# Loading the first channel chunk in DRAM's order and turning it with TensorE, in a mixer kernel on one core

## The chip, the cores and the metric

The kernel runs on one core of one Trainium2 chip. The metric is the device time of one execution in microseconds (us). The kernel before takes 663.87 us, the median of three runs (662.96 to 666.24). About 0.5%, 3.3 us, is what a measurement of this kernel can tell from no change.

The core has a matrix engine (TensorE, PE in the profile, with its weight loads shown apart as PEld), three elementwise engines (VectorE or DVE, ScalarE or ACT, GpSimd or POOL) and SyncE (SP), which here only issues DMAs. ACT and POOL can issue DMAs too. Each engine runs its own instructions in order; they wait for each other through semaphores.

## What is computed

The reference is one block with S = 2048 tokens and D = 640 channels, in float32. Only the first half of it is touched by the change:

```python
mod = (silu(c) @ w_mod).reshape(1, 6, 1, -1)          # sa, ca, ga, sb, cb, gb
h = layernorm(x) * (1 + ca) + sa                      # x = A_q
k_shift = sum over t of k_pad[:, t:t+S, :] * shift_k[:, 3 - t]   # 4 taps, causal, per channel
kv = k_shift * v
y = causal convolution over all 2048 tokens of kv with ssm_k (by FFT), + kv * ssm_D
x = x + ga * (h * y)
x = x + gb * token_mlp(layernorm(x) * (1 + cb) + sb)  # two matrix products over the tokens, gelu between
```

## The kernel before

The 640 channels are worked in five chunks of DC = 128. The long convolution of a chunk is a Fourier transform in two steps, written as matrix products. A token number is 32 * n1 + n2, with n1 below 64 and n2 below 32. Step one sums over n1, so it wants n1 on the partitions, and two halves h of 64 channels fill the 128 partitions: partition 64 * h + n1. The free dimension then holds the 32 values n2 and the 64 channels of that half. `step1` (L211) does that for both sides: side 1 is the filter `ssm_k` (in P, called KSP), side 0 is kv (in X, for the first chunk in X0, which lies in T_y). Each call of step1 handles 8 of 32 channel pairs, 16 matrix instructions of 128 columns, and ScalarE brings the result into T_z (L229). Step two is `f2` (L233): eight groups g, each 32 matrix instructions of 64 columns against W2 (the profile shows each such float32 instruction as two), then ScalarE copies one half out of PSUM (L246) and VectorE multiplies the two spectra in two instructions (`mul`, p<-pst,kt), GpSimd adds (`add`, y<-p). The way back is `i2` (L262) and `i1` (L284), then `gate` (L310).

kv is made from k and v by `kv_ops` (L179): per group of 8 of the n2 values, eight elementwise instructions of 128 x 512, on VectorE or on GpSimd. Groups 0, 2 and 3 of the first chunk are VectorE's and group 1 is GpSimd's.

In the first chunk, k, v and ssm_k are read so that they stand in step one's order at once (`load_k` L130, `load_v` L136, `load_halo` L142, `load_ks` L155). For k and v this makes runs of 64 numbers, 256 bytes, in DRAM; for ssm_k runs of 32 numbers, 128 bytes. `perm_add` (L161) adds ssm_D to the filter's first element on GpSimd, and `perm` (L167) reorders the filter in SBUF on ScalarE, in two instructions (L168).

The order is written out by hand; no scheduler moves anything. The part that matters is L450 to L700. On PE it is: ten warming products without a use (L497), four step1 of the filter, four step1 of kv, eight groups of f2, then, for the first chunk alone and partly for the second one's filter and kv: step1(0, 0), a small transpose, step1(0, 1), i2(0), step1(0, 2), i2(1), step1(0, 3), five `mod_part` (L351, the product with w_mod) and `mod_row` (L362). On VectorE it is: kv groups 0, 2 and 3 of the first chunk, kv groups 0 and 2 of the second chunk, and only then the multiplications of f2, with one instruction of the second chunk's kv group 3 between two of them; behind f2 stand 16 pieces of row statistics (L590, L591) of q. On ScalarE, `w2_part` (L485) spreads the constant W2 from its loaded form, and stands between the step1 and f2 copies.

The second chunk's k goes into KX1, which lies in T_aux; its v goes into VX, where the first chunk's v stood. The second chunk's filter (`load_ks(1)`) goes into KSR, also in T_aux, and because one of the five pieces of w_mod is loaded to the same place (`homes`), load_ks(1) stands behind the third mod_part. SyncE issues nearly all DMAs, in order: the first chunk, the second chunk's k and v between them with two halves of W2, q (into T_x[1], then into T_x[0], where W2's loaded form was), the constant V1, w_mod, then load_ks(1) and the third chunk. A DMA takes one of eight completion semaphores in turn, so an issue also waits for the DMA eight before it.

PSUM is a ring of three slots of 1024 numbers per partition for PE's results, and one more (`tap`).

Of the kernel before, what the change touches and what calls it, by code (L numbers as in the profile page):

```python
# [11 lines left out]
AF = mybir.ActivationFunctionType  # L12
# [8 lines left out]
def _constants():  # L21
# [21 lines left out]
    return {"small": small.astype(np.float32), "w2": w2.reshape(128, 4096).astype(np.float32),  # L43
# [4 lines left out]
def mixer_kernel(ctx: ExitStack, tc: tile.TileContext, q, k, v, shift_k, ssm_k, ssm_D, w1, b1, w2, b2, c,  # L48
                 w_mod, c_small, c_w2, c_v1, out):
# [39 lines left out]
    KX1 = T_aux[:, 0:2240].rearrange("p (n i) -> p n i", i=64)  # L89
# [29 lines left out]
    epsc = small(1)  # L119
# [4 lines left out]
    TAP = tap[:, 512:768].rearrange("p (s i) -> p s i", s=4)  # L124


    kx_of = lambda c: KX1 if c == 1 else KX
    ksr_of = lambda c: T_y[:, 2048:4096] if c == 0 else KSR

    def load_k(c, g, engs=(sync, sync), n=1):  # L130
        for h in range(2):
            r = slice(64 * h, 64 * h + 64)
            engs[h].dma_start(kx_of(c)[r, 3 + 8 * g:3 + 8 * (g + n)],
                           dram(k, 8 * g * D + DC * c + 64 * h, [[32 * D, 64], [D, 8 * n], [1, 64]]))
# [7 lines left out]
    def load_halo(c):  # L142
        for h in range(2):
            sync.dma_start(kx_of(c)[64 * h + 1:64 * h + 64, 0:3],
# [10 lines left out]
    def load_ks(c, upper=sync):  # L155
        for h in range(2):
            (sync, upper)[h].dma_start(ksr_of(c)[64 * h:64 * h + 64].rearrange("p (i n) -> p i n", i=64),
# [3 lines left out]
    def perm_add(c, eng=pool):  # L161
        for h in range(2):
            r = ksr_of(c)[64 * h:64 * h + 1].rearrange("p (i n) -> p i n", i=64)[:, :, 0]
            TT(eng, r, r, DR[64 * h:64 * h + 1], ALU.add)

    def perm(c):
        for i in (slice(0, 16), slice(16, 32)):  # L167
            act.activation(KSP.rearrange("p i (n e) -> p i e n", e=2)[:, i],  # L168
                           ksr_of(c).rearrange("p (i e n) -> p i e n", e=2, i=32)[:, i], AF.Copy)
# [6 lines left out]
    def kv_ops(g, eng=dve, x=X, kx_=KX):  # L176
# [6 lines left out]
        for s in (2, 1, 0):  # L183
# [3 lines left out]
                              pairs(S_), pairs(VX[:, 8 * g:8 * g + 8]), ALU.mult))  # L187
        return ops
# [264 lines left out]
    dve.memset(epsc, EPS)  # L453
    for h in range(2):
        dve.memset(KX[64 * h:64 * h + 1, 0:3, :], 0.0)
        dve.memset(KX1[64 * h:64 * h + 1, 0:3, :], 0.0)
    both = (sync, act)
    load_taps(0, act)
    load_halo(0)
    load_k(0, 0, both)  # L460
    load_k(0, 1, both)
# [3 lines left out]
    load_v(0, 0, both)  # L465
    load_k(0, 2, both)
    load_ks(0, act)
    load_v(0, 2, both)
    load_k(0, 3)
    load_v(0, 1)  # L470
    load_v(0, 3)

    def all_taps():
        for eng, t in ((pool, PW), (dve, TAP)):
            eng.tensor_scalar(t, TR.rearrange("p (i s) -> p s i", s=4), 1.0, None, op0=ALU.mult)
# [17 lines left out]
    all_taps()  # L493
    load_taps(1, pool)
    ps = psum()
    for _ in range(10):
        pe.matmul(ps[:, 0:512], T_in[:, 192:320], T_in[:, 192:704], start=True, stop=True)  # L497
# [898 lines left out]
```

## Time and profile before

| what | before |
| --- | --- |
| median of three runs | 663.87 us (662.96 to 666.24) |
| the profiled execution | 661.6 us, of which 659.8 us from its first to its last instruction |
| PE busy | 614.0 us, 93% |
| VectorE busy | 536.3 us, 81% |
| ScalarE busy | 327.8 us, 50% |
| GpSimd busy | 127.4 us, 19% |
| first f2 matmul begins, last one ends | 34.25 us, 54.5 us |
| first multiplication of f2 on VectorE begins | 40.47 us |
| w_mod's products on PE | 76.05 to 81.6 us |

A row of the timeline says when a stretch of like instructions begins, how long it lasts, its engine and source line, what it writes and reads (out<-in), the shapes, the number of instructions (x), and in brackets how long the engine was idle before it and what ended that. "issue" there means that the engine waited for nothing that the profile shows. Most elementwise instructions have line L57, that of a helper, so their tiles tell them apart.

### The profile page before, as it was taken

To read this page: it belongs to the slowest core of one execution; us is meant where nothing else is said; L and a number is where in the kernel's file an instruction comes from. 1 tells how busy PE (TensorE), PEld (TensorE's weight loads), DVE (VectorE), ACT (ScalarE), POOL (GpSimd) and SP (SyncE) were. 2 spreads that over 40 slices of the span, in tenths; PEclk is the share of its full clock that TensorE was granted. 3 is DMA by queue.
4 is the path that set the end of the run, shared out by engine and by line. 5 is a ranking of instruction groups with operands and counts; after the bars stand their busy time and mean duration, and the time that the engine had idled before them with its cause. 6 is when DMAs were issued, how large, how long until landed. Compare 5 with 4: busy or idle time off the path is not lost.

```text
span 659.8 us, 20943 instructions
## 1 busy us (share of the span) xinstructions
PE 614.0 (93%) x9061; PEld 582.2 (88%) x9061; DVE 536.3 (81%) x930; ACT 327.8 (50%) x534; POOL 127.4 (19%) x143
## 2 busy tenths in 40 slices
PE   6978878999999899878999999999999999999997
PEld 2867567899999897778897999999999999999997
DVE  7798689979899269889979866575899689888895
ACT  0664475746747456477885553345443143333331
POOL 5772048325035044000000000000000520000000
PEclk9999899999999899989999999999999999999999
DMA  9999898465525234160318352245932636346601
GB/s 189 213 252 252 295 185 170 112 111 134 90 68 183 67 99 155 43 142 12 65 33 225 114 147 71 64 123 164 274 92 65 195 105 183 115 120 181 183 30 40
DMA packets 173356, 88.46 MB, mean 134 GB/s; under 512 B 92270, under 2 KB 163472, under 8 KB 173264
## 3 DMA queue, kind: packets, MB, share of 16 engines
q1 hardware_dynamic: 166092, 85.53, 50.6%
q10 hardware_dynamic: 6916, 1.31, 1.1%
q8 instruction: 71, 1.16, 0.7%
q0 software_dynamic: 256, 0.28, 0.2%
q14 instruction: 21, 0.17, 0.1%
HBM read 73.01 MB, written 14.09 MB: 132 GB/s over the span
## 4 chain that ended last, share of the span: by engine, by line
PE 66%; DVE 17%; DMA 5%; ACT 5%; issue 4%; POOL 1%; SPq 1%; ACTq 0%; DVEq 0%; POOLq 0%
PE pst L1250 16%; PE pst L937 12%; PE pst L445 7%; PE pst L1327 7%; PE pst L223 7%; PE pst L271 6%; PE pst L242 6%; DVE p L57 3%; PE pst L291 2%; DVE aux L57 2%; ACT z L280 1%; PE pst L993 1%; DMA y<-in_A_ssm_k_dram 1%; PE tap L351 1%; DVE sm L548 1%
## 5 line engine op out<-in xcount | busy, mean ns | idle before, releaser
L242 PE MATMUL pst<-z,w 128*64 128x64 f32 x2560 | 78.8, 223 | 12.6 <-DVE p L57 6.9
L242 PEld LDWEIGHTS pst<-z,w 128*64 128x64 f32 x2560 | 76.7, 138 | 15.2 <-issue 10.9
L229 ACT ACTIVATE z<-pst 128x1024 f32<-128x1024 f32 (+2 forms) x45 | 43.1, 976 | 38.4 <-PE pst L223 38.3
L57 POOL TENSOR_TENSOR y<-p 128x256 f32<-128x256 f32 x72 | 51.3, 741 | 39.3 <-DVE p L57 39.1
L57 DVE TENSOR_TENSOR p<-pst,kt 128x512 f32<-128x512 f32 x80 | 50.7, 682 | 6.3 <-ACT kt L246 6.3
L271 PEld LDWEIGHTS pst<-v,y 32*128 32x128 f32 x1280 | 38.1, 187 | 5.4 <-issue 4.8
L271 PE MATMUL pst<-v,y 32*128 32x64 f32 x1280 | 40.0, 272 | 2.5 <-issue 2.3
L1250 PE MATMUL pst<-r_z,m_w 128*128 128x320 f32 x222 | 41.6, 309 | 0.1
L246 ACT ACTIVATE kt<-pst 128x512 f32<-128x512 f32 x40 | 23.9, 599 | 34.6 <-PE pst L242 18.3
L57 DVE TENSOR_TENSOR s_w<-s_w,s_w 128x768 fp32r<-128x768 f32 (+1 forms) x26 | 24.6, 947 | 19.1 <-ACT s_w L921 14.3
L223 PE MATMUL pst<-v,p 128*64 128x128 f32 x640 | 36.9, 274 | 3.2 <-ACT p L168 1.8
L921 ACT ACTIVATE s_w<-s_w 128x768 fp32r<-128x768 f32 (+1 forms) x26 | 21.8, 837 | 35.8 <-PE pst L937 12.2
L223 PEld LDWEIGHTS pst<-v,p 128*64 128x64 f32 x640 | 34.8, 137 | 4.8 <-ACT p L168 2.8
L1238 ACT ACTIVATE m_w<-m_v 128x896 fp32r<-128x896 f32 x24 | 22.7, 951 | 32.3 <-PE pst L1250 16.8
L223 PE MATMUL pst<-v,x 128*64 128x128 f32 x512 | 34.5, 291 | 4.1 <-issue 3.3
L57 DVE TENSOR_TENSOR tap<-tap,kt 128x512 f32<-128x512 f32 x51 | 35.5, 697 | 1.3
L223 PEld LDWEIGHTS pst<-v,x 128*64 128x64 f32 x512 | 31.0, 147 | 5.3 <-issue 4.7
L1250 PEld LDWEIGHTS pst<-r_z,m_w 128*128 128x128 f32 x222 | 34.8, 188 | 0.4 <-DVE m_w L57 0.4
L445 PE MATMUL pst<-r_z,wb 128*128 128x320 f32 x180 | 29.7, 323 | 4.2 <-ACT r_z L778 3.1
L445 PEld LDWEIGHTS pst<-r_z,wb 128*128 128x128 f32 x180 | 28.2, 198 | 5.5 <-ACT r_z L778 3.6
L280 ACT ACTIVATE z<-pst 128x512 f32<-128x512 f32 x38 | 20.8, 645 | 23.4 <-PE pst L271 23.4
L57 DVE TENSOR_TENSOR m_w<-m_v,m_w 128x896 fp32r<-128x896 f32 x24 | 27.9, 1167 | 3.3 <-ACT m_w L1238 2.9
(362 smaller groups left out, 1534.1 us busy)
## 6 DMA issues: line engine op xcount, KB each, us to landing
m_x<-xs SPq DMA_DIRECT2D x28, 160.0 KB
out_dram<-m_x SPq DMA_DIRECT2D x28, 160.0 KB
aux<-in_A_ssm_k_dram SPq DMA_DIRECT2D x8, 512.0 KB
m_v<-in_B_w_dram SPq DMA_DIRECT2D x9, 448.0 KB
in<-in_w_mod_dram SPq DMA_DIRECT2D x4, 960.0 KB
x<-in_B_w_dram SPq DMA_DIRECT2D x7, 448.0 KB
s_w<-in_B_w_dram SPq DMA_DIRECT2D x16, 192.0 KB
in<-in_A_v_dram SPq DMA_DIRECT2D x22, 128.0 KB
```

Of the source, the lines that this page charges most:

```text
L57: TT = lambda eng, o, a, b, op: eng.tensor_tensor(o, a, b, op=op)
L223: pe.matmul(ps[64 * ri:64 * ri + 64, o:o + 255:2], lhs, F1[:, 128 * ri:128 * ri + 128], start=True, stop=True)
L229: act.activation(Z[:, side, t, :, k0:k1], ps.rearrange("p (a k e) -> p a k e", a=4, e=2)[:, :, k0:k1], AF.Copy)
L242: pe.matmul(ps[64 * h:64 * h + 64, o:o + 64], W2[k1 // 32][:, 2 * (k1 % 32) + ri], rhs, start=True, stop=True)
L246: act.activation(kt.rearrange("p (m i) -> p m i", i=32), pv[:, :, 1], AF.Copy)
L271: pe.matmul(pp[qd // 2][:, o:o + 64], Y[p, ri, i:i + 2].rearrange("p i k -> p (i k)"), V2[p, 64 * ri:64 * ri + 64], start=ri == 0, stop=ri ...
L280: act.activation(o, i, AF.Copy)
L445: pe.matmul(ps[0:m, h, 0:320], w_.bitcast(F32R), r_[:, 320 * h:320 * h + 320].bitcast(F32R), start=first and i == 0, stop=last and i == 2)
L937: pe.matmul(o, w_.bitcast(F32R), r_.bitcast(F32R), start=first and k == 0, stop=last and k == 2)
L1238: act.activation(W[n][0].bitcast(F32R), A[p, w_], AF.Copy)
L1250: pe.matmul(bank[n], w[:, i].bitcast(F32R), r.bitcast(F32R), start=i == 0 and k == 0, stop=i == 6 and k == 2)
L1327: pe.matmul(acc[s][:, h, 0:320], w[:, f_].bitcast(F32R), u[r + h].bitcast(F32R), start=f_ == 0 and k == 0, stop=f_ == NF - 1 and k == 2)
```

## The change

The first chunk's k, v and ssm_k are loaded in DRAM's order: partition p takes the 16 tokens from 16 * p on, with 128 channels in a run of 512 bytes (`natural`, tiles KN and VN), and the filter's partition is the channel, with its 2048 numbers in a row (tile KSN). They lie in T_x[1] and T_y, not in T_in, so the second chunk's k has its usual tile KX, and the third chunk's filter buffer is no longer shared with k. The taps are loaded as 128 x 512 in place of two times 64 x 256. `kv_natural` is kv_ops in the new layout: the same eight instructions of 128 x 512 for each of the four groups, the last of which now writes over v.

The order that step one wants is then made by TensorE, with a constant TURN (an identity matrix, its even columns and its odd columns, 128 x 256): 64 matrix instructions for the filter, which replace `perm`, and 8 of 512 columns for kv. ScalarE copies both out of PSUM. The warming products are 8 in place of 10. The places of w_mod's pieces are changed, and load_ks(1) is issued behind the first two of them.

```diff
+    def natural(t, src, r, n, row, eng, p0=0, p1=128):
+        eng.dma_start(t[p0:p1, r:r + n], dram(src, (16 * p0 + row) * D, [[16 * D, p1 - p0], [D, n], [1, DC]]))
...
+    act.dma_start(T_rows[:, 0:512], dram(shift_k, 0, [[0, 128], [1, 512]]))
+    natural(KN, k, 3, 4, 0, sync)
+    natural(KN, k, 0, 3, -3, act, 1, 127)
+    natural(KN, k, 0, 3, -3, act, 127, 128)
+    natural(KN, k, 7, 4, 4, sync)
     act.activation(tm[:, 0:1], epsc, AF.Copy)
-    load_D(0, act)
+    sync.dma_start(TURN, c_turn)
+    natural(VN, v, 0, 4, 0, act)
+    sync.dma_start(KSN, dram(ssm_k, 0, [[S, 128], [1, S]]), max_dma_last_dim=2048)
+    act.dma_start(dcol, dram(ssm_D, 0, [[1, 128], [1, 1]]))
+    natural(KN, k, 11, 8, 8, sync)
     sync.dma_start(SM, dram(c_small, 0, [[422, 128], [1, 422]]))
+    natural(VN, v, 8, 4, 8, sync)
+    natural(VN, v, 4, 4, 4, sync)
+    natural(VN, v, 12, 4, 12, sync)
...
-    for _ in range(10):
-        pe.matmul(ps[:, 0:512], T_in[:, 192:320], T_in[:, 192:704], start=True, stop=True)
+    for _ in range(8):
+        pe.matmul(ps[:, 0:512], KN.rearrange("p n i -> p (n i)")[:, 384:512],
+                  KN.rearrange("p n i -> p (n i)")[:, 384:896], start=True, stop=True)
+    ops = kv_natural(1, pool)
+    run(ops[:2])
+    TT(pool, KSN[:, 0:1], KSN[:, 0:1], dcol, ALU.add)
+    run(ops[2:])
+    run(kv_natural(0))
+    run(kv_natural(2))
...
-    perm(0)
+    for b in range(2):
+        ps = psum()
+        for n in range(16):
+            for h in range(2):
+                pe.matmul(ps[64 * h:64 * h + 64, 64 * n:64 * n + 64],
+                          KSN.rearrange("p (n1 n) -> p n n1", n=32)[:, 16 * b + n], TURN[:, 64 * h:64 * h + 64],
+                          start=True, stop=True)
+        act.activation(P.rearrange("p (i n e) -> p n i e", i=32, e=2)[:, 16 * b:16 * b + 16],
+                       ps.rearrange("p (n i e) -> p n i e", n=16, e=2), AF.Copy)
...
     for t in range(4):
         step1(1, t)
     w2_part(0, 0, 0, 32)
+    for b in range(2):
+        ps = psum()
+        for n2 in range(2):
+            for h in range(2):
+                pe.matmul(ps[64 * h:64 * h + 64, 512 * n2:512 * n2 + 512], TURN[:, 128 + 64 * n2:192 + 64 * n2],
+                          VN[:, 8 * b:8 * b + 8, 64 * h:64 * h + 64], start=True, stop=True)
+        for n2 in range(2):
+            n = 16 * n2 + 8 * b
+            act.activation(X0.rearrange("p (i n e) -> p n i e", i=32, e=2)[:, n:n + 8],
+                           ps[:, 512 * n2:512 * n2 + 512].rearrange("p (n i e) -> p n i e", n=8, e=2), AF.Copy)
     for t in range(4):
         step1(0, t, x=X0, last=True)
...
-    homes = [T_v1[:, 2048:3968], T_in[:, 192:2112], T_aux[:, 0:1920], T_in[:, 2240:4160], P[:, 0:1920]]
+    homes = [T_v1[:, 2048:3968], T_aux[:, 2048:3968], T_in[:, 192:2112], T_in[:, 2240:4160], P[:, 0:1920]]
...
                     for kk in range(2):
                         mod_load(0, kk, homes[kk])
+                    load_D(1)
+                    load_ks(1)
...
-                if kk == 2:
-                    load_D(1)
-                    load_ks(1)
```

On PE, from the program's start to the first group of f2, the instructions stood thus before (v is the tile with step one's constant F1, p the filter, y kv, z the result of step one; x16 counts matrix instructions):

```order
L497 MATMUL pst_125<-in 128x512 x10
L223 MATMUL pst_189<-v,p 64x128 x16
L223 MATMUL pst_207<-v,p 64x128 x16
L223 MATMUL pst_225<-v,p 64x128 x16
L223 MATMUL pst_243<-v,p 64x128 x16
L223 MATMUL pst_262<-v,y 64x128 x16
L223 MATMUL pst_281<-v,y 64x128 x16
L223 MATMUL pst_299<-v,y 64x128 x16
L223 MATMUL pst_317<-v,y 64x128 x16
L242 MATMUL pst_376<-z,w_74 64x64 x32
```

and now (xb holds KN, VN and TURN, the y of the second and third row is KSN; step one's line is L241 here, f2's L260):

```order
L516 MATMUL pst_113<-xb 128x512 x8
L533 MATMUL pst_162<-xb,y 64x64 x32
L533 MATMUL pst_196<-xb,y 64x64 x32
L241 MATMUL pst_240<-v,p 64x128 x16
L241 MATMUL pst_258<-v,p 64x128 x16
L241 MATMUL pst_276<-v,p 64x128 x16
L241 MATMUL pst_294<-v,p 64x128 x16
L547 MATMUL pst_313<-xb 64x512 x4
L547 MATMUL pst_320<-xb 64x512 x4
L241 MATMUL pst_327<-v,y 64x128 x16
L241 MATMUL pst_346<-v,y 64x128 x16
L241 MATMUL pst_364<-v,y 64x128 x16
```

The fourth step1 of kv and f2 follow as before. Two blocks of 32 now stand ahead of step one's filter side, and two blocks of 4 between its filter side and its kv side.

On SyncE, behind the loads of q and of the constant V1, the queue read before (rows with in_w_mod are w_mod, aux<-in_A_ssm_k is load_ks(1)):

```order
L528 DMA xa<-in_A_q_dram 64x640 x8
L344 DMA v<-in_w_mod_dram 128x3x640
L344 DMA in<-in_w_mod_dram 128x3x640
L344 DMA aux<-in_w_mod_dram 128x3x640
L344 DMA in<-in_w_mod_dram 128x3x640
L344 DMA p<-in_w_mod_dram 128x3x640
L153 DMA rows<-in_A_ssm_D_dram 1x64 x2
L157 DMA aux<-in_A_ssm_k_dram 64x64x32 x2
```

and reads now:

```order
L566 DMA xa<-in_A_q_dram 64x640 x8
L362 DMA v<-in_w_mod_dram 128x3x640
L362 DMA aux<-in_w_mod_dram 128x3x640
L158 DMA rows<-in_A_ssm_D_dram 1x64 x2
L162 DMA aux<-in_A_ssm_k_dram 64x64x32 x2
L362 DMA in<-in_w_mod_dram 128x3x640 x2
L362 DMA p<-in_w_mod_dram 128x3x640
```

The second chunk's filter has moved ahead of three of the five pieces of w_mod.

More of the change, by code (lines that the diff above doesn't have):

```diff
@@ L187, in kv_ops, with kv_natural @@
                               pairs(S_), pairs(VX[:, 8 * g:8 * g + 8]), ALU.mult))
+        return ops
+    def kv_natural(g, eng=dve):
+        f4 = lambda t: t.rearrange("p (n i) -> p n i", i=128)
+        S_, T_, W_ = (f4(tap[:, 0:512]), f4(KT[0]), TAPN) if eng is dve else (f4(PS_), f4(PT), PWN)
+        w = lambda s: W_[:, None, s, :].to_broadcast([128, 4, 128])
+        kx = lambda s: KN[:, 4 * g + 3 - s:4 * g + 7 - s, :]
+        vx = VN[:, 4 * g:4 * g + 4]
+        ops = [lambda: TT(eng, S_, kx(3), w(3), ALU.mult)]
+        for s in (2, 1, 0):
+            ops.append(lambda s=s: TT(eng, T_, kx(s), w(s), ALU.mult))
+            ops.append(lambda: TT(eng, S_, S_, T_, ALU.add))
+        ops.append(lambda: TT(eng, vx, S_, vx, ALU.mult))
         return ops
@@ L520, in mixer_kernel @@
         w2_part(0, i, 32, 32)
-    run(kv_ops(0, kx_=KX1))
-    run(kv_ops(2, kx_=KX1))
+    run(kv_ops(0))
+    run(kv_ops(2))
     def load_q(js):
@@ L540, in mixer_kernel @@
     load_q(range(12, 16))
-    fill = kv_ops(3, kx_=KX1)
+    fill = kv_ops(3)
     def dv(n):
```

57 lines of the change are left out of this document (21 added, 36 removed).

## The prediction

> **What bounds the kernel now.**
>
> ```profile
> core 0: 659.8 us, clock 0.992
> ...
> PE 614.0 (93%) x9061; PEld 582.2 (88%) x9061; DVE 536.3 (81%) x930; ACT 327.8 (50%) x534; POOL 127.4 (19%) x143
> ```
>
> The granted clock is full almost throughout and PE is busy 93% of the span, so I read first the stretch that the change touches, the first 85 us, and there PE's own timeline. Each row is one stretch of like instructions; an idle time and its end stand in brackets.
>
> ```profile
> 5.53 11.58 PE L497 MATMUL pst<-in 128*128 128x512 f32 x20 [5.53 <-DMA in<-in_A_k_dram]
> ...
> 17.84 7.21 PE L223 MATMUL pst<-v,p 128*64 128x128 f32 x128 [0.74 <-ACT p L168]
> 24.88 5.41 PE L223 MATMUL pst<-v,y 128*64 128x128 f32 x96
> 31.08 1.97 PE L223 MATMUL pst<-v,y 128*64 128x128 f32 x32 [0.79 <-ACT z L229]
> 34.25 5.82 PE L242 MATMUL pst<-z,w 128*64 128x64 f32 x192 [1.20 <-ACT z L229]
> 41.89 4.23 PE L242 MATMUL pst<-z,w 128*64 128x64 f32 x135 [1.83 <-DVE p L57]
> 47.78 3.95 PE L242 MATMUL pst<-z,w 128*64 128x64 f32 x127 [1.65 <-issue]
> 52.62 1.91 PE L242 MATMUL pst<-z,w 128*64 128x64 f32 x58 [0.90 <-issue]
> 54.33 1.97 PE L223 MATMUL pst<-v,x 128*64 128x128 f32 x32
> ```
>
> PE begins f2 at 34.25 and ends it at 54.5, although the grouped view has only 15.9 us of work for it; the rest is waiting. The three waits inside f2 are 1.83 us for VectorE's multiplication and 1.65 and 0.90 us for nothing that is shown, each about 130 records after the last. Why VectorE is late is in its own rows:
>
> ```profile
> 24.63 0.63 DVE L475 TENSOR_SCALAR tap<-rows 128x256 f32<-128x256 f32 x1
> ...
> 34.04 0.70 DVE L57 TENSOR_TENSOR tap<-aux,tap 128x512 f32<-128x512 f32 x1 [2.02 <-DMA aux<-in_A_k_dram]
> ...
> 40.47 1.28 DVE L57 TENSOR_TENSOR p<-pst,kt 128x512 f32<-128x512 f32 x2
> ...
> 55.31 1.29 DVE L57 TENSOR_TENSOR p<-pst,kt 128x512 f32<-128x512 f32 x2 [1.13 <-ACT kt L246]
> ```
>
> Until 24.63 it makes the first chunk's kv, then 16 instructions of the second chunk's, with a wait of 2.02 us for k, and only at 40.47 does it come to f2, whose first group PE had finished about four us earlier. So up to 40 us the bound is VectorE and the DMAs that feed it, and PE has slack. Behind f2 it is PE again:
>
> ```profile
> 62.38 0.43 PE L223 MATMUL pst<-v,x 128*64 128x128 f32 x2
> 64.32 1.91 PE L223 MATMUL pst<-v,x 128*64 128x128 f32 x30 [1.51 <-issue]
> 66.15 3.00 PE L271 MATMUL pst<-v,y 32*128 32x64 f32 x97
> 71.47 1.12 PE L271 MATMUL pst<-v,y 32*128 32x64 f32 x31 [2.32 <-issue]
> 72.51 3.61 PE L223 MATMUL pst<-v,x 128*64 128x128 f32 x32
> 76.05 1.28 PE L351 MATMUL tap<-v,sm 128*32 128x320 f32 x12
> 77.15 1.25 PE L351 MATMUL tap<-in,sm 128*32 128x320 f32 x12
> ```
>
> From 54.33 to the products with w_mod PE has no wait but those two. VectorE, with nothing to do but short pieces for the statistics, then waits for these products:
>
> ```profile
> DVE g L57 <- PE pst L362: 3.1, 1, 3.1
> ...
> 84.80:110.00 25.20, 20.56 (x682) 19.71 (x680) 24.12 (x29) 17.38 (x33) 16.09 (x14) 1.00 0.97 182
> ```
>
> The second row's third number is VectorE's busy time: 24.12 of 25.20 us. From 84.8 on it is full, in lockstep with the rest, so whatever moves the end of PE's work on w_mod moves all that follows by as much. That is the point to which the change must be counted.
>
> **The change, part by part.** I add up PE's new chain from its first instruction to f2's end. The prices are these:
>
> ```profile
> 11.37 0.19 PEld L497 LDWEIGHTS pst<-in 128*128 128x128 f32 x1 [0.24 <-issue]
> ...
> 16.09 0.19 PEld L497 LDWEIGHTS pst<-in 128*128 128x128 f32 x1 [0.24 <-issue]
> ...
> L497 PE MATMUL pst<-in x20: 592/592/1221, 5.5 to 16.5; 128*128 128x512 f32 x20
> ...
> L229 ACT ACTIVATE z<-pst x11: 386/1054/1092, 19.9 to 58.9; 128x1024 f32<-128x1024 f32 x9, 128x256 f32<-128x256 f32 x1, 128x768 f32<-128x768 f32 x1
> ...
> L168 ACT ACTIVATE p<-y 128x1024 f32<-128x1024 f32 x2 | 2.2, 1152 | 11.8 <-DMA in<-in_A_v_dram 11.8
> ...
> L242 PE MATMUL pst<-z,w 128*64 128x64 f32 x512 | 15.9, 223 | 5.6 <-issue 2.5 <-DVE p L57 1.8 <-ACT z L229 1.2
> ...
> L246 ACT ACTIVATE kt<-pst 128x512 f32<-128x512 f32 x8 | 4.8, 598 | 7.1 <-PE pst L242 6.5 <-DVE tap L57 0.4 <-DVE kt L57 0.2
> ```
>
> Warming: 20 records ran from 5.53 to 17.11; the last of them start 0.43 us apart (11 steps from 11.37 to 16.09). Two products fewer are four records, 1.7 us: 15.4. The first k now comes in one transfer with nothing ahead of it on SyncE, which I take as 0.4 us earlier: 15.0, with 14 to 16.5 as bounds.
>
> Filter turn: 64 products of 128 rows, 64 columns of weights and 64 of data, f2's shape. f2 does 192 records in 5.82 us, so 128 take 3.9: 18.9. What the trace does not show is weights taken at every 32nd number; f2's rate is the lower bound, half that rate (3.9 more) the upper. I take f2's rate, since i1 streams its data at such steps without a loss that I can see. ScalarE's copy of the first block lies beside the second; the last one, 1.15 as for L168 today, is exposed: 20.1.
>
> Step one of the filter: 7.2 us for 128 records as before, 27.3. Until then kv is ready: VectorE needs 24 instructions of about 0.72 from about 6 on, 23.3 without waits, and its room to wait is four us; GpSimd, in the same order as before with one addition of one column in place of two rows, is done before that too.
>
> kv turn: four pairs of 512 columns. Whether two products into two halves of the output run side by side is shown by L351: 12 records, six products of 320 columns, take 1.25 us, while one product of 512 takes 0.86 here (two records of 0.43), 0.53 for 320, or 3.2 for six. They do, three at a time. So 4 x 0.86 = 3.4, or 6.9 if pairs went singly; I take 3.4: 30.8. The last two copies, 0.60 each with their hand-over 1.3: 32.1. These are added on a chain on which today nothing stands.
>
> Step one of kv: 7.2 (96 records take 5.41): 39.3. The copy of its first quarter, 0.39 and a hand-over of 0.1 to 0.2: f2 begins at about 39.9, where today it begins at 34.25.
>
> f2: VectorE has by then made 16 more instructions, from 24.6 to 36.6 without the wait, since the second chunk's k no longer waits behind so many short runs. It has 3 us to spare, so f2 runs at PE's pace, 15.7 to 15.9 us: 55.6, against 54.33. That is 1.3 us later, if nothing interrupts. The gaps named "issue" come about every 130 records in f2, so f2 will meet three or four again. Today those of 1.65 and 0.90 are paid. I take 1.5 us on a queue that is a little emptier, with 0 and 4.4 (today's three gaps together) as ends. f2 ends 2.8 us later.
>
> Behind f2 the order is unchanged, so the gaps of 1.51 and 2.32 us and the slow step1 behind the second stay.
>
> The DMAs: the first chunk's loads shrink from some 16,800 runs of 128 and 256 bytes to some 5,400 of 512 bytes and more, while the bytes grow from 3.4 to 3.8 MB. What runs of 512 bytes are worth is shown where two loads of w1 with such runs are alone:
>
> ```profile
> GB/s 0 0 0 0 0 0 0 0 0 20 105 72 67 177 292 346 338 305 230 210 202 200 187 192 210 233 228 230 205 202 200 205 205 182 118 64 21 0 0 0
> ...
> 12.00:16.00 4.00, 4.00 (x10) 1.71 (x9) 3.79 (x7) 0.00 (x0) 2.45 (x3) 1.00 1.35 225
> 68.00:72.00 4.00, 1.68 (x62) 1.66 (x58) 3.86 (x14) 0.00 (x0) 0.00 (x0) 1.00 1.03 394
> ```
>
> About 200 to 230 GB/s, the last column's 225 of today's first chunk at 128 and 256 bytes; only long runs reach 394. So k and v gain nothing, ssm_k in runs of 2 KB does: 2.2 MB at 0.215 and 1.6 MB at 0.35 are 15 us in place of 16 to 18. [...]
>
> load_ks(1) was no loss where it stood: GpSimd waited for it with nothing else to do, and ScalarE comes to that filter (L168) only at 90.19:
>
> ```profile
> POOL aux L57 <- DMA aux<-in_A_ssm_k_dram: 9.2, 2, 7.0
> ...
> 90.19 2.19 ACT L168 ACTIVATE p<-aux 128x1024 f32<-128x1024 f32 x2
> 76.00:80.00 4.00, 4.00 (x47) 1.88 (x48) 3.33 (x7) 2.02 (x6) 1.38 (x2) 1.00 0.46 177
> ```
>
> Its 1 MB, 4.7 us at 0.215, now goes ahead of three pieces of w_mod, whose DMAs were through at about 77.5 (share 0.46 in the last row). With 1 to 3 us won at the head they land at 79 to 81, and PE wants the third at 78.2 + 2.8 = 81 (two of 1.1 behind the first at 76.05). I take nothing for it; without the head's gain it would be about 1 us.
>
> Sum: 661.6 + 2.8 = 664.4 for an execution like the profiled one, which lies 2.3 us under the median of the runs. So the forecast for the median is 664.4 + 2.3 = 666.7 us, 0.43% more: within the 0.5% that a measurement of this kernel can tell from no change, though at its edge.
>
> **The rivals.** *Slower, through the gaps.* Today VectorE's lateness hides part of PE's interruptions in f2; when f2 is bound by PE each is paid in full. With today's three, 1.3 + 4.4 = 5.7: 669.6 us. It decides once f2's idle time on PE passes 2 us. For it speaks that they recur by count of records; against it, that the queue is lighter.
>
> *Slower, through a late filter.* If ssm_k lands after 17.3, with PE warm and idle for over 2.3 us, PE falls to half clock, as behind the gap of 2.32 us (32 records in 3.61 instead of 1.97, and a granted clock of 0.54 in the row below). That is 2.3 of waiting and some 1.8 of slow work, with the 2.8 together 6.9: 670.8. Ahead of its end lie about 2.3 MB, which at 200 to 250 GB/s are through by 12 to 14 us, so it is unlikely.
>
> ```profile
> 72.40:76.10 3.70, 3.70 (x41) 3.38 (x41) 0.21 (x2) 3.46 (x6) 0.00 (x0) 0.54 1.04 394
> ```
>
> [...]
>
> *Faster, through the gaps behind f2.* If the emptier queue takes away 1.51 and 2.32 and with them the slow step1 (1.64), 5.5 us go: 661.6 + 1.3 - 5.5 + 2.3 = 659.7. For it speaks that gaps fall where the DMA share is about 1; against it, that w_mod and now ssm_k stand in the queue just there, at a share of 1.03.
>
> **How the numbers follow.** Forecast 0.42, the gaps 0.28, the late filter 0.10, faster 0.20. So faster by over 0.5% is 0.20, within 0.5% 0.42, slower 0.38. The range takes in the two large rivals, 659.7 and 669.6, and the slow turn of the filter in part: 659.5 to 672.
>
> **What would show it.** Right: f2's first record near 40, VectorE idle for some 3 us or more ahead of its first p<-pst,kt, f2 without waits for VectorE, w_mod's products at 78 to 80 instead of 76.05. Wrong: f2 before 37, filter blocks longer than 2.2 us each, kv blocks longer than 2 us each, or PE's gaps behind f2 gone.

## The result, and the profile after

The changed kernel is slower: 672.84 us in the median of nine runs (669.69 to 677.66), against 663.89 us for nine runs of the kernel before. The ratio is 1.0128, with a 95% interval of 1.009 to 1.0166, so some 9 us are lost where the forecast had 2.8, and the range ended at 672. The profiled execution took 669.69 us (before 661.6), of which 667.9 are span. A few executions of some kernels ran slow at a lower granted clock, one as long as 1028.5 us at 0.555; medians count them, ratios leave them out.

The span and the busy times on the profile's page, for the changed kernel:

```profile
span 667.9 us, 21211 instructions
...
PE 624.9 (94%) x9201; PEld 591.9 (89%) x9201; DVE 537.2 (80%) x929; ACT 330.0 (49%) x538; POOL 128.3 (19%) x142
```

PE is busy 10.9 us longer than before, and the other engines hardly at all. So the loss shows as busy time of PE, and PE's own timeline is the view to read. It is the one that the prediction read before; L533 is the filter turn, L547 the kv turn, L241 step one, L260 f2, L369 the products with w_mod:

```profile
7.47 9.48 PE L516 MATMUL pst<-xb 128*128 128x512 f32 x16 [7.47 <-DMA xb<-in_A_k_dram]
16.88 8.05 PE L533 MATMUL pst<-xb,y 128*64 128x64 f32 x128
26.09 8.75 PE L241 MATMUL pst<-v,p 128*64 128x128 f32 x128 [1.16 <-ACT p L536]
34.67 3.60 PE L547 MATMUL pst<-xb 128*64 128x512 f32 x16
39.47 7.21 PE L241 MATMUL pst<-v,y 128*64 128x128 f32 x128 [1.20 <-ACT y L551]
47.16 13.53 PE L260 MATMUL pst<-z,w 128*64 128x64 f32 x442 [0.48 <-ACT z L247]
...
62.88 3.58 PE L260 MATMUL pst<-z,w 128*64 128x64 f32 x70 [2.19 <-issue]
66.15 2.31 PE L241 MATMUL pst<-v,x 128*64 128x128 f32 x32
...
86.57 1.28 PE L369 MATMUL tap<-v,sm 128*32 128x320 f32 x12
```

Three rows are not as foretold. The first k lands at 7.47, where it landed at 5.53 before. The filter turn takes 8.05 us for 128 records (two for each of its 64 products), where f2 takes 3.9 for as many of the same shape. And the filter side of step one takes 8.75 us instead of 7.21. The kv turn (3.60), both waits for ScalarE's last copies (1.16 and 1.20) and the kv side of step one (7.21) are as the sum had them. f2 begins at 47.16, 12.9 us later than before and 7.3 later than forecast.

The view of one line's instructions shows that the turn's weights are what is slow; the numbers are the shortest, median and longest of one, in ns:

```profile
L533 PEld LDWEIGHTS pst<-xb,y x128: 204/218/238, 16.9 to 24.6; 128*64 128x64 f32 x128
L533 PE MATMUL pst<-xb,y x128: 275/285/342, 16.9 to 24.6; 128*64 128x64 f32 x128
```

The windows view has the granted clock in the third column from the right, and behind it the DMA share and the GB/s:

```profile
8.00:12.00 4.00, 4.00 (x6) 1.45 (x5) 3.58 (x6) 0.00 (x0) 3.67 (x5) 1.00 1.09 347
17.00:21.00 4.00, 4.00 (x68) 4.00 (x68) 3.83 (x6) 0.00 (x0) 3.76 (x4) 1.00 1.29 214
20.00:25.00 5.00, 4.93 (x80) 4.79 (x78) 4.76 (x7) 1.19 (x2) 4.84 (x5) 1.00 1.16 284
25.00:30.00 5.00, 3.91 (x44) 3.91 (x46) 4.79 (x7) 1.39 (x2) 4.69 (x5) 0.66 1.07 182
47.10:60.00 12.90, 12.84 (x426) 12.72 (x428) 9.54 (x16) 10.43 (x14) 7.19 (x10) 1.00 0.49 155
```

During the turn the clock was full, so the turn is not slow through the clock. Step one behind it is: 0.66 is a third of full clock lost over 5 us, one stretch of about 3.4 us at half. The last row is f2 up to 60 us: there the DMA engines are busy only half the time (0.49), and 442 records run without a pause.

VectorE, which was late for f2 before, now waits for it:

```profile
50.42 1.29 DVE L58 TENSOR_TENSOR p<-pst,kt 128x512 f32<-128x512 f32 x2 [10.24 <-ACT kt L264]
```

It idles 10.24 us ahead of its first multiplication. The bound in the first 47 us has gone over from VectorE to PE, as the prediction said, only much further. From 86.57 on (before 76.05) everything follows 10.5 us later: f2 of the second chunk begins at 111.28 against 100.65, of the third at 158.58 against 147.92, of the fourth at 202.47 against 191.52. Then 3.3 us come back, at a pause that PE's timeline of the kernel before has in the fourth chunk:

```profile
223.34 3.29 PE L223 MATMUL pst<-v,x 128*64 128x128 f32 x30 [1.84 <-issue]
```

It cost 1.84 us and some 1.4 of slow work behind it (the 30 records take 3.29 us, where 32 take 1.97 at full clock); the changed kernel pauses 0.21 us there. So f2 of the fifth chunk is 7.6 us late (246.64 against 239.00), and the execution ends 8.1 late.

### The profile page after: what moved, and what is told of

Its sections match the earlier page's. It is cut to its first block, busy times and chain, and to the rows that moved or that the text cites. A ratio compares the mean times of both kernels' runs of the same rounds, so it can differ in the third digit from the quotient of the medians.

```text
span 667.9 us, 21211 instructions
## 1 busy us (share of the span) xinstructions
PE 624.9 (94%) x9201; PEld 591.9 (89%) x9201; DVE 537.2 (80%) x929; ACT 330.0 (49%) x538; POOL 128.3 (19%) x142
## 4 chain that ended last, share of the span: by engine, by line
PE 72%; DVE 17%; ACT 4%; issue 3%; DMA 2%; SPq 0%; DVEq 0%; ACTq 0%
PE pst L1287 16%; PE pst L974 11%; PE pst L241 10%; PE pst L463 7%; PE pst L1364 7%; PE pst L260 7%; PE pst L289 6%; DVE p L58 3%; PE pst L309 2%; PE pst L516 1%; DVE aux L58 1%; DVE tap L58 1%; PE pst L1030 1%; PE pst L533 1%; PE tap L369 1%
## 5 line engine op out<-in xcount | busy, mean ns | idle before, releaser
L260 PE MATMUL pst<-z,w 128*64 128x64 f32 x2560 | 80.3, 225 | 9.5 <-DVE p L58 4.7
L260 PEld LDWEIGHTS pst<-z,w 128*64 128x64 f32 x2560 | 78.1, 140 | 12.1 <-issue 8.3
L241 PE MATMUL pst<-v,p 128*64 128x128 f32 x640 | 38.5, 281 | 1.9 <-ACT p L536 1.2
L58 DVE TENSOR_TENSOR s_w<-s_w,s_w 128x768 fp32r<-128x768 f32 (+1 forms) x26 | 24.6, 947 | 18.1 <-ACT s_w L958 13.4
L241 PEld LDWEIGHTS pst<-v,p 128*64 128x64 f32 x640 | 36.3, 141 | 2.7 <-ACT p L536 1.3
L241 PE MATMUL pst<-v,x 128*64 128x128 f32 x512 | 32.5, 283 | 0.5 <-DVE p L58 0.4
L241 PEld LDWEIGHTS pst<-v,x 128*64 128x64 f32 x512 | 29.6, 143 | 1.3 <-issue 0.6
```

The lines of the kernel that those rows point to most:

```text
L58: TT = lambda eng, o, a, b, op: eng.tensor_tensor(o, a, b, op=op)
L241: pe.matmul(ps[64 * ri:64 * ri + 64, o:o + 255:2], lhs, F1[:, 128 * ri:128 * ri + 128], start=True, stop=True)
L260: pe.matmul(ps[64 * h:64 * h + 64, o:o + 64], W2[k1 // 32][:, 2 * (k1 % 32) + ri], rhs, start=True, stop=True)
```

## The experiments

The theories: **S**, the filter turn is slow because its weights are read at every 32nd number; **T**, the first k is late because the taps' load, one row of 2 KB sent to all 128 partitions, goes ahead of it; a drop of the clock behind the waits as the third loss; and against them that the queue, the load order or the kv turn is to blame. Each kernel below is the changed kernel with one edit, unless it says otherwise.

### The turn's weights side by side

```diff
-  KSN.rearrange("p (n1 n) -> p n n1", n=32)[:, 16 * b + n], TURN[:, 64 * h:64 * h + 64],
+  KSN[:, 64 * (16 * b + n):64 * (16 * b + n) + 64], TURN[:, 64 * h:64 * h + 64],
```

The same 128 records, but each product takes 64 neighbouring numbers as weights, so the filter is used in another order than the reference's.

> The changed kernel, but the 64 products that turn the filter take 64 neighbouring numbers as weights instead of every 32nd; the filter's numbers then stand in another order, so this computes a convolution with a shuffled filter. Theory S (the step of 128 bytes between weights halves the turn's pace): the 128 records take 3.9 to 4.1 us instead of 8.05, and with PE busy at full pace ahead of the 1.16 us wait the half clock behind it (step one of the filter in 8.75 us) goes too, to 7.2; f2 then begins at about 41.6 instead of 47.16 and the time falls by about 5 us. Theory C (the turn is slow for another reason, a slow clock or the switch between products): 8 us remain, f2 begins near 47 and the time stays within 1 us.

PE's timeline, and the instructions of the turn:

```profile
7.39 9.21 PE L516 MATMUL pst<-xb 128*128 128x512 f32 x16 [7.39 <-DMA xb<-in_A_k_dram]
16.53 3.95 PE L533 MATMUL pst<-xb,y 128*64 128x64 f32 x128
21.64 7.21 PE L241 MATMUL pst<-v,p 128*64 128x128 f32 x128 [1.16 <-ACT p L536]
...
41.19 9.78 PE L260 MATMUL pst<-z,w 128*64 128x64 f32 x315 [0.49 <-ACT z L247]
...
109.66 9.55 PE L260 MATMUL pst<-z,w 128*64 128x64 f32 x320 [0.49 <-ACT z L247]
```

```profile
L533 PEld LDWEIGHTS pst<-xb,y x128: 132/138/139, 16.5 to 20.2; 128*64 128x64 f32 x128
```

The turn takes 3.95 us, the very price that the prediction used, with a weight load at 138 ns instead of 218. The clock did not drop behind it (1.00 from 21 to 30 us), although the wait is the same 1.16. f2 begins 6.0 us earlier than in the changed kernel: 4.1 from the turn, 1.5 from the clock, 0.35 from an earlier start. The median is 667.1 us, ratio to before 1.0035 (1.0005 to 1.0066), where the forecast's was 666.7 to 663.87, or 1.0043. S holds: the turn is slow through the step of its weights. The interval lies clear below the changed kernel's (1.009 to 1.0166; each ratio is to the kernel before measured beside it), so in the medians the slow turn, with the drop that goes with it, is worth some 6 us.

That this median lies so near the forecast is in part luck. In the profiled execution, 668.05 us, w_mod's products begin at 81.38, 5.3 us later than before and not 2.8, and of the 6.0 us that f2 gained 1.6 are left at the second chunk's f2 (109.66 against 111.28). From 70 to 80 us the granted clock was 0.68, with a pause of 3.13 us at its start, where the changed kernel's trace has 0.85; then PE waited 0.90 us for w_mod, and behind that `mod_row` took 3.15 us and 235 records of i1 5.95, against 2.29 and 3.71 there. So what the turn costs in the whole time rests on the medians, not on one pair of traces.

### A step of 132 bytes instead of 128

```diff
+    KSN = T_aux[:, 0:2112].rearrange("p (n1 n) -> p n1 n", n=33)[:, :, 0:32]
...
-  KSN.rearrange("p (n1 n) -> p n n1", n=32)[:, 16 * b + n], TURN[:, 64 * h:64 * h + 64],
+  KSN[:, :, 16 * b + n], TURN[:, 64 * h:64 * h + 64],
```

The filter is loaded into rows of 33 numbers, to see whether it is the round step that hurts or any wide one (W).

> The changed kernel with the filter stored in rows of 33 numbers in place of 32, so that the turn's weights stand 132 bytes apart and not 128; its load then goes in runs of 128 bytes. Theory B (a step of exactly 128 bytes falls on the same part of the memory each time): the turn's 128 records take 4 us, as with neighbours. Theory W (any step wider than a few numbers halves the pace): 8 us, as in the changed kernel. The load is slower, so the time itself says little.

```profile
18.27 7.79 PE L533 MATMUL pst<-xb,aux 128*64 128x64 f32 x128 [1.03 <-POOL aux L58]
```

7.79 us: W, as far as these two steps go. The step need not be a round one to cost the factor of two; steps between 4 and 128 bytes were not tried. One execution took 670.18 us.

### ScalarE orders the filter first

```diff
+    KSM = T_aux[:, 0:2048].rearrange("p (n n1) -> p n n1", n=32)
+    for b in range(2):
+        act.activation(KSM[:, 16 * b:16 * b + 16],
+                       KSN.rearrange("p (n1 n) -> p n n1", n=32)[:, 16 * b:16 * b + 16], AF.Copy)
...
-  KSN.rearrange("p (n1 n) -> p n n1", n=32)[:, 16 * b + n], TURN[:, 64 * h:64 * h + 64],
+  KSM[:, 16 * b + n], TURN[:, 64 * h:64 * h + 64],
```

> The changed kernel, but ScalarE first copies the filter into the order n2, n1 (two instructions of 128 x 1024 into a free stretch of T_aux), so that the turn's weights are neighbours and the result is the same as before. Theory S: the copies lie in ScalarE's idle time, end at about 15.8, a little before PE is through with warming at 17, so f2 begins at about 41.6 as in the kernel with neighbouring weights, and the time falls by about 5 us. Theory C: f2 begins at 47 or later, the time is the same or up to 1 us more.

PE's timeline, then ScalarE's:

```profile
17.40 3.95 PE L536 MATMUL pst<-xb,aux 128*64 128x64 f32 x128
...
42.02 2.02 PE L260 MATMUL pst<-z,w 128*64 128x64 f32 x61 [0.48 <-ACT z L247]
```

```profile
13.50 3.92 ACT L531 ACTIVATE aux<-y 128x1024 f32<-128x1024 f32 x2 [9.28 <-POOL y L58]
```

The turn is quick again, in a kernel that computes what the changed one does: 667.74 us, ratio 1.0051 (1.0019 to 1.0083), again below the changed kernel's. The copies that make it so take 3.92 us for the two, where the kernel before reordered as much in 2.2, from runs of 32 numbers (L168): reading at a wide step is slow there too. They lie beside PE's warming, and the turn does not wait for them.

### The taps behind the first k

```diff
-    act.dma_start(T_rows[:, 0:512], dram(shift_k, 0, [[0, 128], [1, 512]]))
     natural(KN, k, 3, 4, 0, sync)
     natural(KN, k, 0, 3, -3, act, 1, 127)
     natural(KN, k, 0, 3, -3, act, 127, 128)
+    act.dma_start(T_rows[:, 0:512], dram(shift_k, 0, [[0, 128], [1, 512]]))
```

> The changed kernel, with the load of the taps (one row of 2 KB read for all 128 partitions) behind the three rows of k ahead of the chunk in ScalarE's queue, not in front. Theory T (this load holds up the first k, which now lands at 7.4 us and not at 5.5): PE's warming begins at 5.5 to 6 and f2 begins 1.5 us sooner, while VectorE's first product waits for the taps and begins no sooner. Theory K (256 KB of k in runs of 512 bytes are themselves that slow at the start): warming begins at 7.2 or later and nothing moves.

```profile
4.87 9.09 PE L516 MATMUL pst<-xb 128*128 128x512 f32 x16 [4.87 <-DMA xb<-in_A_k_dram]
15.48 8.30 PE L533 MATMUL pst<-xb,y 128*64 128x64 f32 x128 [1.53 <-POOL y L58]
24.93 7.21 PE L241 MATMUL pst<-v,p 128*64 128x128 f32 x128 [1.14 <-ACT p L536]
```

The first k lands at 4.87 instead of 7.47: T holds. But only 1.4 us of the 2.6 reach the turn, since PE now waits for GpSimd's addition of ssm_D, to which GpSimd comes later because it waits for the taps too. VectorE gets its taps later and starts kv at 10.25 instead of 8.24. The median is 670.88 us, ratio 1.0068 (1.0021 to 1.0114), which overlaps the changed kernel's: what T costs in the whole time is not settled. The clock did not drop here either (1.00 from 21 to 30 us).

### The wait filled, and the changed kernel once more

To see whether the 1.16 us wait drops the clock, two products without a use are put into it:

```diff
+    ps = psum()
+    for w_ in (512, 128):
+        pe.matmul(ps[:, 0:w_], KN.rearrange("p n i -> p (n i)")[:, 384:512],
+                  KN.rearrange("p n i -> p (n i)")[:, 384:384 + w_], start=True, stop=True)
```

> The changed kernel, with two products without a use (512 and 128 columns, about 1.07 us) behind the filter's turn, which fill PE's wait of 1.16 us for ScalarE's copy. Theory G (the idle wait of 1.16 us makes the clock fall for 3.4 us): step one of the filter takes 7.2 us instead of 8.75 and f2 begins 1.4 us sooner, at about 45.8. Theory U (the turn at half pace itself makes the clock fall, the wait has no part): step one stays at 8.7 and f2 begins at 47.2 or later.

```profile
23.76 1.35 PE L540 MATMUL pst<-xb 128*128 128x512 f32 x4
25.04 7.21 PE L241 MATMUL pst<-v,p 128*64 128x128 f32 x128
```

Step one takes 7.21 us, as the theory wanted, but it does so above with the wait kept as well, so this shows little. The median is 671.59 us, ratio 1.0112 (1.0072 to 1.0152). The changed kernel was therefore profiled a second time, unedited:

> The changed kernel once more, unchanged, for the half-clock stretch behind the 1.16 us wait for the filter's copy. If the wait causes the drop by its length, step one of the filter takes about 8.7 us again and f2 begins at 47; if the drop hangs on chance (when the wait falls), it takes 7.2 us, as in the five experiments with the same wait, and f2 begins at about 45.7. The gap inside f2 of about 2.2 us should come again behind some 442 records in either case.

```profile
17.22 8.07 PE L533 MATMUL pst<-xb,y 128*64 128x64 f32 x128
26.45 8.87 PE L241 MATMUL pst<-v,p 128*64 128x128 f32 x128 [1.16 <-ACT p L536]
...
47.63 15.43 PE L260 MATMUL pst<-z,w 128*64 128x64 f32 x512 [0.48 <-ACT z L247]
...
84.46 1.36 PE L369 MATMUL tap<-in,sm 128*32 128x320 f32 x12 [0.96 <-DMA in<-in_w_mod_dram]
86.84 1.35 PE L369 MATMUL tap<-in,sm 128*32 128x320 f32 x12 [1.01 <-DMA in<-in_w_mod_dram]
89.85 1.28 PE L369 MATMUL tap<-p,sm 128*32 128x320 f32 x12 [1.66 <-DMA p<-in_w_mod_dram]
```

The drop comes again: 8.87 us, at a granted clock of 0.68 from 25 to 30 us. So it belongs to this kernel in two executions of two. Yet with a wait of 1.13 to 1.16 us at the same place it is missing in all the other kernels here that kept it (7.21 us each), four of which have the slow turn as well. The length of the wait alone does not explain that, and two executions against nine are few to rule out chance; the cause of these 1.5 us stays open. The gap of 2.19 us inside f2 did not come again, against the expectation: f2 ran 512 records without a pause, and PE was at w_mod's products 5.4 us sooner. It then waited 3.63 us there for w_mod, and the second chunk's f2 began at 111.27, as in the first trace (111.28). The two executions are 0.1 us apart in the whole, though PE lost its time in different places.

### The second chunk's filter behind w_mod

```diff
                     for kk in range(2):
                         mod_load(0, kk, homes[kk])
-                    load_D(1)
-                    load_ks(1)
...
             for kk in range(2, 5):
                 mod_load(0, kk, homes[kk])
+            load_D(1)
+            load_ks(1)
```

> The changed kernel with the second chunk's filter loaded behind all five pieces of w_mod, not ahead of three of them. The prediction took its place as free: the time stays within 0.5 us and PE's wait for the last piece (0.5 us) goes. Rival: the 1 MB in runs of 128 bytes ahead of w_mod is what makes PE's gaps behind f2 (2.80 us) and the wait for w_mod, and the time falls by 2 us or more.

```profile
46.49 13.73 PE L260 MATMUL pst<-z,w 128*64 128x64 f32 x442 [0.48 <-ACT z L247]
...
87.42 2.33 PE L369 MATMUL tap<-in,sm 128*32 128x320 f32 x24
89.57 1.25 PE L369 MATMUL tap<-p,sm 128*32 128x320 f32 x12
```

No wait for w_mod is left. The second chunk's f2 began at 110.77, half a microsecond sooner. The median is 671.1 us and the ratio 1.0092 (1.0051 to 1.0133), which overlaps that of the changed kernel: how much the order of these loads costs in it is not settled. That it is not free once PE comes sooner shows in the waits: in all seven traces with this load ahead of w_mod in which PE came to the products before 86.57, it waited for w_mod there, 0.81 to 3.63 us in all; in the three with the load behind, it never did.

### Each half of the change alone

Onto the kernel before, the filter's load and turn only, with kv as it was:

```diff
-    load_ks(0, act)
+    sync.dma_start(KSN, dram(ssm_k, 0, [[S, 128], [1, S]]), max_dma_last_dim=2048)
...
-    perm(0)
+    for b in range(2):
+        ps = psum()
...
```

> The kernel before with the filter's part of the change alone: ssm_k loaded in rows of 2048 numbers and turned by 64 products with weights at every 32nd number; k, v, the warming and all else as before. If the turn on PE's chain is what costs: the turn takes 8 us from about 17 on, step one of the filter begins near 26.4 instead of 17.84, f2 near 41.5 instead of 34.25 and ends 3 to 5 us later, and the time rises by 3 to 5 us. If instead the kv part costs and the filter's shorter loads help: f2 begins by 37 at the latest, VectorE reaches f2 before 39 and the time falls by 1 to 2 us.

PE's timeline, and VectorE's:

```profile
17.27 8.05 PE L516 MATMUL pst<-xb,y 128*64 128x64 f32 x128
26.47 7.21 PE L225 MATMUL pst<-v,p 128*64 128x128 f32 x128 [1.15 <-ACT p L519]
...
41.15 2.37 PE L244 MATMUL pst<-z,w 128*64 128x64 f32 x73 [0.48 <-ACT z L231]
...
78.64 1.71 PE L353 MATMUL tap<-v,sm 128*32 128x320 f32 x12
```

```profile
44.41 1.29 DVE L58 TENSOR_TENSOR p<-pst,kt 128x512 f32<-128x512 f32 x2 [5.72 <-ACT kt L248]
```

The slow turn is there without the rest of the change, at the same 8.05 us, which clears kv's loads, the load order and the kv turn of it. f2 begins 6.9 us late, but w_mod's products only 2.6. Of the difference 1.9 us are f2 itself, 18.2 us long up to the next step one (59.33) instead of 20.1, since VectorE is no longer late but waits 5.72 us; the other 2.4 come back behind f2. 668.63 us, ratio 1.006 (1.0024 to 1.0096): the 3 to 5 us that were expected if the turn is what costs.

The other half: the changed kernel with the filter loaded and reordered as before.

```diff
-    sync.dma_start(KSN, dram(ssm_k, 0, [[S, 128], [1, S]]), max_dma_last_dim=2048)
+    for h in range(2):
+        (sync, act)[h].dma_start(KSN[64 * h:64 * h + 64].rearrange("p (i n) -> p i n", i=64),
+                                 dram(ssm_k, 64 * h * S, [[32, 64], [S, 64], [1, 32]]))
...
-    for b in range(2):
-        ps = psum()
...
+    for i in (slice(0, 16), slice(16, 32)):
+        act.activation(KSP.rearrange("p i (n e) -> p i e n", e=2)[:, i],
+                       KSN.rearrange("p (i e n) -> p i e n", e=2, i=32)[:, i], AF.Copy)
```

> The changed kernel with the filter loaded and reordered as before (two loads in runs of 128 bytes, two copies by ScalarE, no turn on PE), so that only k and v are loaded in DRAM's order and turned. If the filter's turn is the main cost: step one of the filter begins near 17.5, f2 near 38 to 39, held by VectorE's kv, which in the changed kernel ends at 27, and the time is 665 to 667, 1 to 3 us above before. If the kv part is the main cost: f2 begins at 43 or later and the time stays within 2 us of the changed kernel's.

PE's timeline, and GpSimd's addition of ssm_D:

```profile
20.57 8.87 PE L241 MATMUL pst<-v,p 128*64 128x128 f32 x128 [4.88 <-ACT p L534]
...
82.98 1.35 PE L369 MATMUL tap<-in,sm 128*32 128x320 f32 x12 [0.81 <-DMA in<-in_w_mod_dram]
85.78 2.36 PE L369 MATMUL tap<-p,sm 128*32 128x320 f32 x12 [1.45 <-DMA p<-in_w_mod_dram]
```

```profile
18.57 0.77 POOL L58 TENSOR_TENSOR y<-y,rows 1x64 f32<-1x64 f32 x2 [6.29 <-DMA rows<-in_A_ssm_D_dram]
```

A miss: 672.1 us where 665 to 667 were expected, with a wide interval (ratio 1.0032 to 1.0201, four runs). The trace shows two waits that I had not counted. GpSimd waits 6.29 us for ssm_D, whose load stands behind half of the filter's short runs in ScalarE's queue, and adds it only at 18.57; ScalarE's reordering follows, and PE waits 4.88 us and then takes 8.87 us for step one, where others took 7.21. And PE, which was at w_mod's products only 2.7 us later than before, waited 2.3 us for w_mod there, with the second chunk's filter ahead of it in the queue. The second chunk's f2 begins 7.6 us late (108.27 against 100.65). So this half alone does not show the kv turn's price by itself.

### Versions built from the findings

The first has the ordered copy, the taps behind k, the second chunk's filter behind w_mod, and, as its one new edit, ScalarE in place of GpSimd adding ssm_D:

```diff
-    TT(pool, KSN[:, 0:1], KSN[:, 0:1], dcol, ALU.add)
+    act.activation(KSN[:, 0:1], KSN[:, 0:1], AF.Identity, bias=dcol)
```

> The changed kernel with what the runs so far point to: ScalarE adds ssm_D and copies the filter into the order n2, n1 before the turn, the taps are loaded behind the rows of k ahead of the chunk, and the second chunk's filter is loaded behind w_mod. Chain theory: warming from 4.9 to 14, turn from 15 to 19, f2 from about 40, which is still 6 us later than before, and the time is 665 to 667, above before. If the stride, the taps and the filter's place were all that costs, the time is 661 or less.

```profile
14.53 4.03 PE L536 MATMUL pst<-xb,aux 128*64 128x64 f32 x128 [1.21 <-ACT aux L531]
19.72 7.21 PE L241 MATMUL pst<-v,p 128*64 128x128 f32 x128 [1.16 <-ACT p L539]
...
39.26 5.70 PE L260 MATMUL pst<-z,w 128*64 128x64 f32 x188 [0.49 <-ACT z L247]
```

f2 begins at 39.26, where the prediction had 39.9. 665.12 us, ratio 1.0017 (0.9983 to 1.0052): the same as before. The second loads the filter right behind the first k, lets the copy read in order and write at a wide step, and spreads VectorE's last kv group of the second chunk one f2 group sooner:

```diff
-            dv(-(-len(fill) // max((6 if c else 8) - g, 1)))
+            dv(-(-len(fill) // max((6 if c else 7) - g, 1)))
```

> The kernel v1_best with the filter and ssm_D loaded right behind the first rows of k, the copy that reorders the filter reading its numbers in order and writing at steps of 256 bytes, and the second chunk's kv group 3 finished one group of f2 sooner. If PE's chain sets the time: the copies take 2.2 to 2.5 us in place of 3.95, the turn begins at 13.4 (the end of warming) in place of 14.5, the wait of 0.95 us behind f2 goes, w_mod's products end 2 us sooner than in v1_best, and the time is 662.5 to 664.5, the same as before. If the copy also halves its pace at steps in the writes, it gains 1 us only.

```profile
8.43 3.80 ACT L531 ACTIVATE aux<-y 128x1024 f32<-128x1024 f32 x2
```

The copies are as slow when they write at 256-byte steps (3.80 us for the two). 665.44 us, ratio 1.0015 (0.998 to 1.005): not under the first version, and above the 662.5 to 664.5 that were expected. The third is the kernel before with the filter part alone, ordered by ScalarE, and the same spreading:

> The kernel before with the filter's part alone as in b1_filter_alone, but with ScalarE's addition and copy into n2, n1 ahead of the turn, and kv group 3 of the second chunk finished one group of f2 sooner. The turn takes 4 us in place of 8.05, f2 begins at 37 to 37.5 in place of 41.15, VectorE, which in b1 was free at 38.7, is no longer waited for, and the time is 2 to 4 us under b1_filter_alone's, 663 to 666. If less than 1 us comes back, b1's loss was not the turn.

```profile
17.23 4.00 PE L519 MATMUL pst<-xb,z 128*64 128x64 f32 x128 [0.80 <-ACT z L514]
...
37.05 6.05 PE L244 MATMUL pst<-z,w 128*64 128x64 f32 x200 [0.49 <-ACT z L231]
```

664.44 us, ratio 1.0007 (0.9973 to 1.0042), in the 663 to 666 that were expected and 4.2 us under the filter's half with its slow turn. No version is faster than the kernel before.

## Why the prediction was wrong

The mechanism was right up to f2: the chain on PE grows, and VectorE falls off the critical path. That what moves w_mod's products moves the rest by as much held in the profiled execution; in the second one PE came there 5.4 us sooner than in the first and won nothing by it, since it then waited 3.63 us for w_mod and was slow behind that (`mod_row` in 3.41 us and 235 records of i1 in 5.16, against 2.29 and 3.71 in the first). The sizes were wrong, and one of them by a choice between two bounds.

**The filter turn** is the step that failed: "I take f2's rate, since i1 streams its data at such steps without a loss that I can see". It took 8.05 us, not 3.9; the upper bound of 7.8 was the right end. The row it was taken from was about data that is streamed, and the operand in question was weights. With neighbouring weights the same records took 3.95. That is 4.1 of the 7.3 us by which f2 began late, and the sign "filter blocks longer than 2.2 us each" appeared at 4.0. The traces give the size: 218 ns for a weight load at steps of 128 bytes, 213 at 132, 138 side by side.

**Warming's end**, 15.0 with bounds to 16.5, was 16.95. "One transfer with nothing ahead of it on SyncE" was true of SyncE's queue, but the taps' load on ScalarE's queue, now 256 KB in place of 128, went ahead on the DMA engines. Behind it the first k lands at 7.47, ahead of it at 4.87. That is 1.9 us.

**Step one of the filter**, "7.2 us as before", took 8.75 and 8.87 at a lower clock (0.66 and 0.68 from 25 to 30 us): 1.5 us that the sum had only in the rival of a late filter. The filter was not late; the rival's place was wrong, and its cause is open.

**The kv turn, the copies and kv's step one** were right: 3.60 for 3.4, 1.16 and 1.20 for 1.15 and 1.3, 7.21 for 7.2. Pairs of 512 columns ran side by side: one after the other they had been priced at 6.9.

**f2 and its gaps**: 15.7 and 1.5 were forecast, 17.2 together. The profiled run took 19.0, with one gap of 2.19 and a tail of 70 records in 3.58 us at half clock, where they take 2.26 at full. The second execution had no gap and took 16.4 with a wait for VectorE. So the rival of the gaps was there once, inside its bounds, and with a half clock behind it that it lacked. Behind f2 the stretch to w_mod's products was 20.4 us in place of 21.7 in the profiled run: nearly unchanged, as the sum had it. In the second execution it was 17.1, 4.6 less, which is most of the 5.5 of the faster rival; the 3.63 us of waits for w_mod, and slow work behind them, took that back. That rival had left out that w_mod must have landed for the gain to reach the end.

**The DMAs**: the queue moved 347 GB/s at 8 to 12 us, when by the order of its loads the filter's 2-KB rows were in it, and 214 at 17 to 21, with the runs of 512 bytes. Both are near the 0.35 and 0.215 of the sum, and the turn did not wait for the filter. **load_ks(1)** "nothing" held in the profiled run only because PE was 10 us late: w_mod's last piece had landed by 91.0. Where PE came sooner it waited, 2.3 us with kv's half alone and 3.6 us in the second execution, the two longest. The pieces did not land at "79 to 81"; the last came at 85.8 and 89.9 in these two.

Of the 10.5 us at w_mod's products in the profiled run 7.3 are thus the head and 1.8 f2, less 1.3 given back behind it, on top of the forecast's 2.8. The result lies 0.84 us above the range, which had taken in the slow turn only "in part". The rival of the gaps with the turn at its upper bound would have been 669.6 + 3.9 = 673.5; a range up to there would have held the result, but only in part for the right reasons: the late first k and the half clocks are in none of these terms.

## What to carry to other kernels

Price an unknown operand by the row of the same operand: the turn was put at 3.9 us since i1's data at such steps showed no loss that I could see; with weights at them it took 8.05. When two bounds differ by a factor of two and no row lies between, carry the dear one into the range in full. And count slack once: the filter's half alone made f2 begin 6.9 us later and the second chunk's f2 3.1 (103.70 against 100.65); the whole change made it 12.9 and 13.4 later in its two executions, and the second chunk's f2 10.6 in both. The slack that hid 3.8 us of the first delay hid no more of the larger one; how much of that is the new order of the loads is not separated. And compare medians, not single executions: pauses and half-clock stretches move single points of a trace by several us (w_mod's products by 5.4 between the two of the changed kernel).

## What the runs showed of the hardware

- Float32 weights of 64 numbers at steps of 128 or 132 bytes load in 213 to 218 ns instead of 138, and the products behind them run at half the pace (8.05 and 7.79 us for 128 records, against 3.95).
- Two of ScalarE's copies of 128 x 1024 numbers take 3.92 to 3.95 us when they read SBUF at 128-byte steps and 3.80 when they write it at 256-byte steps, against 2.2 for the reordering in runs of 32 numbers.
- One row of 2 KB loaded to all 128 partitions ahead of the first large load holds that up by 1.8 to 2.8 us: the first k lands at 6.67 to 7.52 in the eight traces with the taps ahead, and at 4.76 to 4.90 in the three with them behind.
- In the traces of the kernel before and of the changed kernel each half-clock stretch of the first 300 us lasts 3.41 us, and within a trace they begin whole multiples of 3.41 us apart: at 72.50, 222.69 and 284.12 before (44 and 18 of them apart), at 25.88, 63.43, 77.08 and 292.12 in the changed kernel (11, 4 and 63). There the first begins inside the wait of 1.16 us, which lasts from 24.93 to 26.09, and the second 0.55 us after the pause of 2.19 us ended. Of six pauses of 2.16 to 2.22 us inside f2, two were followed by slow work (the changed kernel, 70 records in 3.58 us; the filled wait, 74 in 3.73), and four were not (70 records in 2.26 to 2.31 us: the taps behind k, the filter behind w_mod, 132 bytes, kv's half). Of eleven waits of 1.13 to 1.16 us ahead of the filter's step one, two went with a drop (8.75 and 8.87 us, both executions of the changed kernel) and nine did not (7.21).
- The pauses of PE for which the profile shows no wait have fixed places. In all 14 traces those of the first 110 us (0.2 to 3.4 us long) stand, within two, behind record 477, 604, 731, 858, 984, 1111, 1238, 1491 or 1620 of PE: whole multiples of 127 records apart, whatever PE does there and at whatever time. Not every such place pauses in every execution. What PE waits for there, no run shows.
